# Linear attention and a Mish feed-forward: q loaded whole by halves of the heads, later loads and weight stores rearranged, two PSUM banks swapped

## The chip, the cores and the metric

The kernel runs on one core of one Trainium2 chip. The time is device microseconds of one execution; the median over several executions counts. Between two kernels, 0.3% is about what a measurement of this kernel can tell.

## The reference

q, k and v are float32, 8 batches by 8 heads by 576 positions by 64. The attention has no softmax; each head's 64 x 64 product of k and v is applied to q, and each row is divided by its root mean square. The result, as 4608 tokens by 512, goes through a feed-forward layer. Its weights w_in (512 x 2048) and w_out (2048 x 512) come as float64; all else is float32.

```
kv  = einsum('bhsd,bhse->bhde', k, v)
out = einsum('bhsd,bhde->bhse', q, kv)
x   = out / sqrt(mean(out*out, -1) + 1e-6) * g_norm
x   = x.transpose(0, 2, 1, 3).reshape(4608, 512)
h   = x @ w_in
sp  = where(h > 20, h, log1p(exp(min(h, 20))))
g   = h * tanh(sp)
return g @ w_out
```

## The kernel before

**The two large products.** x @ w_in and g @ w_out are each computed block by block as a scheme of seven products in place of eight (PROD, L22): the left operand has seven forms (A11, S1, S2, S4, A12, S3, A22, sums and differences of its quarters), the weights have seven (T1, T3, T2, T4, B11, B21, B22). Every form is split into a high and a low part in the reduced float32 type fp32r (split, L120 to L122: ScalarE casts the high part, VectorE subtracts to get the low one), and each product is three matmuls. Tokens go in 9 tiles of 512. A tile of part one has 28 slots, 7 products times 4 groups of columns; mm_in (L526) issues a slot's matmuls and put_in (L545) adds up the results, applies Mish (ScalarE, L118) and stores g to DRAM (gd) from GpSimd's queue. Part two reads g back (g_load, L731), makes its forms (g_form, L748) and multiplies them by w_out's (mm_out, L771). Its first half tile is different: its seven products go by pairs of chunks into four banks of their own (L855 to L875).

**Weights.** The float64 words are converted on the chip. weight_forms (L128) returns seven steps that the order calls by number: LOAD, SCALE (ScalarE, L142), JOIN (three VectorE operations, L147 to L149), DIFF (L157 to L159), BLOCKS and SUMS (the splits), and STORE. w_in's forms stay in SBUF as wf0 to wf7. w_out's are made in 16 halves during part one: weight_out (L192) converts one half in the tile wst, which has one buffer, and stores it (L200) to DRAM, in wod. In part two they are read back, as wo_load (L727).

**The order.** Nothing is scheduled automatically. The program text sets each engine's order: plan and evict are tables of calls by slot number (at, then, slot, L474 to L488), and the head of the kernel, which prepares the first tile, is written out (L592 to L648). SP issues nearly all loads in that order and waits in order; its transfers use eight lanes (DMAHW0 to 7 in the lists below), and an issue waits for the transfer that used the lane eight before. GpSimd's have eight of their own (DMASW).

**The head.** Tokens of the first tiles are handled by two units of four heads (u = 0 and 1). rows_load (L293) loads q, transpose (L318) turns it on TensorE, turned (L336) copies it to SBUF, kv_first_product (L228) and kv_keep (L266) make the k and v product, project (L354) applies it, sums (L391), rstd (L409) and normalize (L431) do the norm. rows[0] holds four consecutive tokens per partition, so that a run is 1 KB; spots (L289) picks the partitions of a segment.

## Time and profile before

| | |
|---|---|
| runs of the kernel | 878.30, 880.26, 880.67 us, median 880.26 |
| profiled execution | 880.55 us |
| its span, first to last instruction | 878.8 us |
| mean granted clock of TensorE | 0.987 |
| TensorE busy | 835.3 us, 95%, 7132 matmuls |
| VectorE busy | 608.8 us, 69% |
| ScalarE busy | 465.0 us, 53% |
| GpSimd busy | 78.5 us, 9% |
| moved by DMA | 175.54 MB, mean 200 GB/s |

The profile is of one execution. Busy times are shares of the span; an engine's idle time counts only where another waits for it. Start times in the timeline are microseconds from the span's start, and a bracket at a row's end gives the idle time of that engine just before it and the instruction whose end released it. The granted clock is given as a share of the full 2.4 GHz: 0.50 is 1.2 GHz.

### The profile page before, as it was taken

The numbers are of one execution on the slowest core, as the hardware profiler recorded it, in microseconds if no ns is written. First come the engines' busy times: TensorE is split into PE (matmuls) and PEld (weight loads), VectorE is DVE, ScalarE is ACT, GpSimd is POOL, SyncE is SP. The second block draws the span as 40 slices with busy tenths as digits, with TensorE's granted clock in tenths as the row PEclk, the third lists the DMA queues.
The fourth block names the chain that finished last, engine by engine and source line by source line (L and its number), as shares of the span: only waits on it lengthen the run. The fifth ranks groups of instructions, "written<-read, shape, count | busy, mean of one in ns | idle before, by whom it ended". The sixth has DMA issues, their size and how long they took to land.

```text
span 878.8 us, 17412 instructions
## 1 busy us (share of the span) xinstructions
PE 835.3 (95%) x7132; PEld 804.6 (92%) x7132; DVE 608.8 (69%) x804; ACT 465.0 (53%) x703; POOL 78.5 (9%) x133
## 2 busy tenths in 40 slices
PE   4679998999999999999999989999999999999997
PEld 4467998989999999999899979999999999999997
DVE  3899666877777686777763577677666777776772
ACT  3677666655665757666665443444444334334441
POOL 2001111111111111111112100000000000000000
PEclk9999999999999999999999989999999999999999
DMA  9964887979878695858377992444444443344421
GB/s 311 255 195 137 241 254 238 296 234 277 272 218 279 210 291 173 279 171 243 138 235 293 422 399 81 149 151 149 124 129 135 121 120 121 120 123 148 151 62 48
DMA packets 140320, 175.54 MB, mean 200 GB/s; under 512 B 16272, under 2 KB 117648, under 8 KB 139216
## 3 DMA queue, kind: packets, MB, share of 16 engines
q1 hardware_dynamic: 129232, 136.67, 50.7%
q0 software_dynamic: 11008, 37.76, 11.4%
q8 instruction: 56, 0.92, 0.4%
q14 instruction: 24, 0.20, 0.1%
HBM read 112.39 MB, written 62.00 MB: 198 GB/s over the span
## 4 chain that ended last, share of the span: by engine, by line
PE 73%; ACT 8%; DVE 7%; DMA 6%; issue 4%; SPq 1%; ACTq 0%; DVEq 0%
PE a L775 22%; PE bc L775 17%; PE a L532 16%; PE bc L532 11%; PE s L252 2%; DMA wf<-wod 2%; DMA wod<-wst 1%; DVE fa L122 1%; DVE ur L553 1%; DMA wf<-in_q_dram 1%; PE q L871 1%; ACT L417 1%; ACT L118 1%; DVE gf L385 1%; PE x L329 1%
## 5 line engine op out<-in xcount | busy, mean ns | idle before, releaser
L775 PE MATMUL a<-wf,gf 128*128 128x256 f32 x1632 | 201.8, 283 | 0.5 <-DVE ur L814 0.5
L775 PEld LDWEIGHTS a<-wf,gf 128*128 128x128 f32 x1632 | 198.4, 192 | 0.7 <-DVE ur L814 0.7
L122 DVE TENSOR_TENSOR gf<-g,gf 128x1024 fp32r<-128x1024 f32 (+1 forms) x123 | 132.9, 1087 | 92.5 <-ACT gf L121 92.4
L532 PE MATMUL a<-gf,wf 128*128 128x256 f32 x1296 | 174.1, 288 | 11.1 <-DVE gf L435 4.6
L532 PEld LDWEIGHTS a<-gf,wf 128*128 128x128 f32 x1296 | 163.8, 194 | 18.2 <-DVE gf L435 5.4
L532 PE MATMUL bc<-gf,wf 128*128 128x256 f32 x1296 | 171.6, 285 | 0.1
L532 PEld LDWEIGHTS bc<-gf,wf 128*128 128x128 f32 x1296 | 162.5, 192 | 1.9 <-DVE gf L122 0.7
L121 ACT CAST gf<-g 128x1024 fp32r<-128x1024 f32 (+1 forms) x123 | 114.5, 939 | 86.9 <-DVE g L755 65.5
L775 PE MATMUL bc<-wf,gf 128*128 128x256 f32 x1224 | 152.4, 283 | 0.0
L775 PEld LDWEIGHTS bc<-wf,gf 128*128 128x128 f32 x1224 | 149.3, 192 | 0.0
L532 PE MATMUL a<-a,wf 128*128 128x256 f32 x432 | 59.3, 287 | 0.8 <-DVE ur L553 0.8
L532 PEld LDWEIGHTS a<-a,wf 128*128 128x128 f32 x432 | 55.5, 193 | 3.8 <-DVE ur L553 1.0
L118 ACT ACTIVATE ur<-ur 128x1024 f32<-128x1024 f32 x36 | 38.1, 1058 | 37.1 <-DVE ur L553 37.1
L122 DVE TENSOR_TENSOR fa<-fl,fh 128x1024 fp32r<-128x1024 f32 x28 | 34.2, 1222 | 18.4 <-ACT fh L121 16.3
L122 DVE TENSOR_TENSOR gf<-gf 128x512 fp32r<-128x512 f32 x45 | 30.4, 689 | 24.0 <-ACT gf L121 24.0
L121 ACT CAST gf<-a 128x1024 fp32r<-128x1024 f32 x17 | 17.9, 1050 | 53.8 <-DVE a L752 53.8
L121 ACT CAST gf<-gf 128x512 fp32r<-128x512 f32 x45 | 27.1, 619 | 33.2 <-DVE gf L456 19.1
L509 ACT COPY ur<-a 128x512 f32<-128x512 f32 (+1 forms) x53 | 27.3, 516 | 32.6 <-PE a L775 26.5
L556 POOL DMA_DIRECT2D gd<-ula x36 | 26.3, 731 | 190.6 <-ACT ula L118 139.5
L553 DVE TENSOR_TENSOR ula<-bc,ula 128x512 f32<-128x512 f32 x36 | 24.7, 687 | 24.1 <-PE bc L532 23.9
L500 ACT COPY ur<-bc 128x512 f32<-128x512 f32 (+1 forms) x53 | 27.5, 518 | 26.4 <-PE bc L775 24.9
L551 POOL DMA_DIRECT2D gd<-ulb x36 | 25.6, 712 | 116.0 <-ACT ulb L118 104.6
(141 smaller groups left out, 937.0 us busy)
## 6 DMA issues: line engine op xcount, KB each, us to landing
g<-gd SPq DMA_DIRECT2D x18, 2048.0 KB, 15.7
gd<-ur POOLq DMA_DIRECT2D x36, 512.0 KB, 4.8
wod<-wst SPq DMA_DIRECT2D x16, 896.0 KB, 9.9
wf<-wod SPq DMA_DIRECT2D x8, 1792.0 KB
gd<-ula POOLq DMA_DIRECT2D x36, 256.0 KB, 5.0
gd<-ulb POOLq DMA_DIRECT2D x36, 256.0 KB, 4.5
w<-in_moe_w_out_dram SPq DMA_DIRECT2D x32, 256.0 KB, 5.9
km<-in_k_dram SPq DMA_DIRECT2D x28, 256.0 KB, 3.4
```

The lines of the kernel that those rows point to most:

```text
L118: nc.scalar.activation(o, i, AF.Mish)
L121: nc.scalar.copy(hi, src)
L122: nc.vector.tensor_sub(lo, src, hi.bitcast(F32))
L252: nc.tensor.matmul(kvps[o * D:(o + 1) * D, b % 2, h0 // 2 + i, :], kt, vt, start=(c == 0), stop=(c == CM))
L329: nc.tensor.matmul(ps[a][o * D:(o + 1) * D, c * P:(c + 1) * P], src, ident, start=True, stop=True)
L500: then(t + 2, lambda: nc.scalar.copy(dst(st, "22"), st["c"]))
L509: then(t + 4, lambda: nc.scalar.copy(dst(st, "12"), st["a"]))
L532: nc.tensor.matmul(bank[:, jj], w[:, right, a, kc, :], xf[:, b, kc, :], start=first and jj == kc == s == 0, stop=(kc == 1 and s == 2), ski ...
L551: at(t + 2, lambda: eng.dma_start(left[:, :, TH:T], o))
L553: nc.vector.tensor_add(o, bank, o)
L556: at(t + 3, lambda: eng.dma_start(left[:, :, 0:TH], o))
L775: nc.tensor.matmul(bank, gf[:, a, c, :], wo[c][:, right, b, :], start=first and c == s == 0, stop=(c == NF2 - 1 and s == 2), skip_group_ch ...
```

## The change

1. q of the first two tiles is laid out by whole blocks of 128 tokens, one token per partition and block. A transfer then has runs of 64 values; for the first tile there are four per half of the heads (rows_load takes the block c and the heads). The transposes become eight whole 128 x 128 ones per unit in place of sixteen of half the width, and project reads contiguous columns. The output rows of these tiles are stored 128 at a time.
2. The order of the head: q's second half and the second halves of k and v are issued ahead of the second weights; the second unit's transposes follow the first k and v product; the third weights' JOIN stands after the second unit's normalization; in part one's first slots the form S3 and kv_keep change places.
3. The banks of the first norm's sums and of the second unit's projection are exchanged ("a" and "bc").
4. w_out's forms are kept in DRAM and SBUF as two halves of 128 columns, the half outermost. A half is then one contiguous run of 7168 bytes per partition, and it is stored from GpSimd's queue in place of SP's. In part two each matmul's moving operand is two runs of 128 columns.
5. The load of g for the second half tile is issued behind the last two blocks of w_out's forms.

```diff
-    wod = [tc.dram_tile([P, 7, 2, G], F32, name=f"wod{c}") for c in range(NF2)]
+    wod = [tc.dram_tile([P, 2, 7, 2, P], F32, name=f"wod{c}") for c in range(NF2)]
...
-            nc.sync.dma_start(wod[c][:, :, :, h * P:(h + 1) * P], f.rearrange("p f s m n -> p f s (m n)").bitcast(F32))
+            nc.gpsimd.dma_start(wod[c][:, h], f.rearrange("p f s m n -> p f s (m n)").bitcast(F32))
...
-    def rows_load(j):
+    def rows_load(j, c, h0, n):
         for b, s0, cols in segments(j):
-            p = spots(cols)
-            src = q[b, 0:1, s0:s0 + 1, :]
-            src = bass.AP(src.tensor, src.offset, [[TR * D, p.stop - p.start], [S * D, H], [1, TR * D]])
-            nc.sync.dma_start(rows[j][p], src)
+            t0, t1 = max(cols.start, c * P), min(cols.stop, (c + 1) * P)
+            if t0 < t1:
+                src = q[b, h0:h0 + 1, s0 + t0 - cols.start:s0 + t0 - cols.start + 1, :]
+                src = bass.AP(src.tensor, src.offset, [[D, t1 - t0], [S * D, n], [1, D]])
+                nc.sync.dma_start(rows[j][t0 - c * P:t1 - c * P, c, h0 * D:(h0 + n) * D].rearrange("p (h d) -> p h d", d=D), src)
...
+                    h = 4 * u + 2 * a
                     for c in range(TR):
-                        for o in range(2):
-                            src = rows[j][:, 4 * u + 2 * a + o, c * D:(c + 1) * D]
-                            nc.tensor.matmul(ps[a][o * D:(o + 1) * D, c * P:(c + 1) * P], src, ident, start=True, stop=True)
+                        nc.tensor.transpose(ps[a][:, c * P:(c + 1) * P], rows[j][:, c, h * D:(h + 2) * D], ident)
...
-                st["x"] = [bank_new("a").rearrange("p m t -> p (m t)") for _ in range(2)]
+                st["x"] = [bank_new("bc").rearrange("p m t -> p (m t)") for _ in range(2)]
...
-                    ps = bank_new("bc").rearrange("p m t -> p (m t)") if u == 0 else ps_t.tile([P, T], F32, name="ss") if a == 0 else kvps.rearrange("p b n d -> p (b n d)")
+                    ps = bank_new("a").rearrange("p m t -> p (m t)") if u == 0 else ps_t.tile([P, T], F32, name="ss") if a == 0 else kvps.rearrange("p b n d -> p (b n d)")
...
-    rows_load(0)
+    for c in range(TR):
+        rows_load(0, c, 0, 4)
     kv0 += [wfp.tile([P, NKC, 9 * D], F32, name=f"wf{n}") for n in (3, 4)]
     kv_first(first)
+    for c in range(TR):
+        rows_load(0, c, 4, 4)
+    kv_first(second)
     weights(1, LOAD)
-    kv_first(second)
...
-    for f, n in ((S2, 0), (A12, 1), (S4, 2), (S3, 3), (A22, 5)):
+    for f, n in ((S2, 0), (A12, 1), (S4, 2), (S3, 4), (A22, 5)):
...
-    at(4, lambda: kv_keep(1, slice(0, NKC)))
+    at(3, lambda: kv_keep(1, slice(0, NKC)))
...
-        wo[c] = wfp.tile([P, 7, 2, G], F32R, name=f"wf{c}")
+        wo[c] = wfp.tile([P, 2, 7, 2, P], F32R, name=f"wf{c}")
...
-                    bank, gf[:, a, c, :], wo[c][:, right, b, :],
+                    bank, gf[:, a, c, :], wo[c][:, :, right, b, :],
...
-    at(t8 + 26, lambda: g_load(1))
...
     at(t, lambda: [wo_load(c) for c in range(NF2 - 2, NF2)])
+    at(t, lambda: g_load(1))
```

The lists below give an engine's instructions in program order: the line, the operation, written tile, read tiles and shape, how often in a row, and, in brackets, whom it waits for.

SP in the head, before: wf_139 of q goes whole, and the second weights (wf_145) stand ahead of the second halves of k and v.

```order
L137 DMA w_136<-in_moe_w_in_dram 128x4x256 x2
L298 DMA wf_139<-in_q_dram 128x8x256
L226 DMA wf_141<-in_k_dram 128x2x576
L226 DMA wf_142<-in_v_dram 128x2x576
L137 DMA wf_145<-in_moe_w_in_dram 128x4x256 x2
L226 DMA wf_141<-in_k_dram 128x2x576
L226 DMA wf_142<-in_v_dram 128x2x576 [waits DMAHW0_49]
```

The same with the change:

```order
L137 DMA w_136<-in_moe_w_in_dram 128x4x256 x2
L295 DMA wf_139<-in_q_dram 128x4x64 x4
L226 DMA wf_144<-in_k_dram 128x2x576
L226 DMA wf_145<-in_v_dram 128x2x576
L295 DMA wf_139<-in_q_dram 128x4x64 [waits DMAHW0_49]
L295 DMA wf_139<-in_q_dram 128x4x64 [waits DMAHW1_49]
L295 DMA wf_139<-in_q_dram 128x4x64 [waits DMAHW2_49]
L295 DMA wf_139<-in_q_dram 128x4x64 [waits DMAHW3_49]
L226 DMA wf_144<-in_k_dram 128x2x576 [waits DMAHW4_49]
L226 DMA wf_145<-in_v_dram 128x2x576 [waits DMAHW5_49]
L137 DMA wf_154<-in_moe_w_in_dram 128x4x256 [waits DMAHW6_49]
L137 DMA wf_154<-in_moe_w_in_dram 128x4x256 [waits DMAHW7_49]
```

Eight issues of q stand where one did, and the second weights (here wf_154) come behind all of k, v and q of the first tile.

VectorE in the head, before: from the second weights' differences (L157 to L159) past the first unit's normalization (L435, of x) and the third weights' JOIN (wf_152) to the second unit's normalization (L435, of the banks a).

```order
L157 TENSOR_TENSOR wd<-fl 128x512
L158 TENSOR_TENSOR wd<-fl,wd 128x256
L159 TENSOR_TENSOR wd<-fl,wd 128x256
L122 TENSOR_TENSOR wf_290<-fl,wf_290 128x256
L122 TENSOR_TENSOR wf_290<-fl,wf_290 128x2x256
L122 TENSOR_TENSOR wf_290<-wd,wf_290 128x4x256
L435 SCALAR_TENSOR_TENSOR gf<-x_281,gcol,fa 128x512 x2
L122 TENSOR_TENSOR gf<-gf 128x512
L147 TENSOR_SCALAR fl<-fl 128x1024
L148 SCALAR_TENSOR_TENSOR fl<-wf_152,fl 128x1024
L149 SCALAR_TENSOR_TENSOR fl<-wf_152,fl 128x1024
L435 SCALAR_TENSOR_TENSOR gf<-a,gcol,fh 128x512 x2
```

With the change, whose lines are lower by five (L430 is the normalization, wf_154 holds the second weights' words), the end of the second weights' JOIN and what follows:

```order
L149 SCALAR_TENSOR_TENSOR fl<-wf_154,fl 128x1024
L430 SCALAR_TENSOR_TENSOR gf<-x_267,gcol,fa 128x512 x2
L157 TENSOR_TENSOR wd<-fl 128x512
L158 TENSOR_TENSOR wd<-fl,wd 128x256
L159 TENSOR_TENSOR wd<-fl,wd 128x256
```

and some rows further, from the second weights' last splits to the third weights' JOIN (wf_159):

```order
L122 TENSOR_TENSOR gf<-gf 128x512
L122 TENSOR_TENSOR wf_332<-wd,wf_332 128x4x256
L430 SCALAR_TENSOR_TENSOR gf<-bc,gcol,fh 128x512 x2
L448 TENSOR_TENSOR s_125<-gf 128x512
L449 TENSOR_TENSOR gf<-gf 128x2x256
L122 TENSOR_TENSOR gf<-s_125,gf 128x512
L147 TENSOR_SCALAR fl<-fl 128x1024
L148 SCALAR_TENSOR_TENSOR fl<-wf_159,fl 128x1024
L149 SCALAR_TENSOR_TENSOR fl<-wf_159,fl 128x1024
```

The first unit's normalization moved ahead of the second weights' differences, and the third weights' JOIN moved from ahead of the second unit's normalization to behind it.

SP at the boundary of the parts, before: g is a half tile's Mish result read back, wf6 and wf7 (here wf_5905 and wf_5907) are the last two blocks of w_out's forms.

```order
L729 DMA wf_5722<-wod_107 128x3584 [waits PE_49]
L729 DMA wf_5843<-wod_108 128x3584 [waits PE_49]
L729 DMA wf_5845<-wod_109 128x3584 [waits PE_49]
L734 DMA g<-gd_95 128x16x256 [waits DMASW7_49,DMASW5_49,DMAHW6_49,DMASW2_49,Pool_49]
L729 DMA wf_5905<-wod_110 128x3584 [waits DMAHW7_49,PE_49]
L729 DMA wf_5907<-wod_111 128x3584 [waits DMAHW0_49,PE_49]
```

With the change:

```order
L723 DMA wf_5823<-wod_109 128x3584 [waits DMASW7_49,DMASW3_49,PE_49]
L723 DMA wf_5881<-wod_110 128x3584 [waits DMASW5_49,DMASW1_49,PE_49]
L723 DMA wf_5883<-wod_111 128x3584 [waits DMASW7_49,DMAHW1_49,DMASW3_49,PE_49]
L728 DMA g<-gd_95 128x16x256 [waits DMAHW2_49,Pool_49]
L728 DMA g<-gd_96 128x16x256 [waits DMASW4_49,DMAHW3_49,DMASW0_49,DVE_49]
```

The second load of g moved from ahead of the last two blocks to behind them. GpSimd's queue, with the change, around the first two stores of w_out's forms, which before were on SP:

```order
L551 DMA gd_96<-ula 128x2x256 [waits DMASW6_49,Activation_49]
L200 DMA wod_104<-wst 128x1792 [waits DMASW7_49,DVE_49]
L554 DMA gd_96<-ur 128x1024 [waits DMASW0_49]
L546 DMA gd_96<-ulb 128x2x256 [waits DMASW1_49,Activation_49]
L551 DMA gd_96<-ula 128x2x256 [waits DMASW2_49,Activation_49]
L200 DMA wod_104<-wst 128x1792 [waits DMASW3_49,DVE_49]
```

A store stands behind the store of g from ula and ahead of the one from ur, and waits for VectorE.

## Rows read from the trace of the kernel before

**Rows 1.** Waits of ScalarE: who, for whom, us in total, times, longest.

```profile
ACT wst L121 <- DMA wod<-wst: 9.4, 2, 5.0
```

**Rows 2.** Timeline of the head, TensorE and VectorE (start, us, engine, line, operation).

```profile
10.90 3.68 PE L329 MATMUL x<-ident,wf 128*64 128x128 f32 x32 [10.90 <-DMA wf<-in_q_dram]
...
36.73 0.49 PE L532 MATMUL a<-gf,wf 128*128 128x256 f32 x1 [4.56 <-DVE gf L435]
...
21.33 0.69 DVE L147 TENSOR_SCALAR fl<-fl 128x1024 uint32<-128x1024 uint32 x1 [2.21 <-ACT fl L142]
...
29.68 1.41 DVE L435 SCALAR_TENSOR_TENSOR gf<-x,gcol,fa 128x512 f32<-128x512 f32 x2 [1.16 <-ACT fa L414]
32.20 0.69 DVE L122 TENSOR_TENSOR gf<-gf 128x512 fp32r<-128x512 f32 x1 [1.10 <-ACT gf L121]
```

**Rows 3.** Windows: us, busy (instructions) of PE, PEld, DVE, ACT, POOL; PEclk, DMA share, GB/s.

```profile
2.00:17.00 15.00, 6.10 (x64) 6.13 (x64) 6.30 (x9) 4.03 (x6) 5.09 (x20) 1.00 0.99 335
36.00:66.00 30.00, 23.09 (x216) 20.32 (x216) 27.78 (x43) 19.50 (x30) 0.75 (x1) 0.89 0.67 205
129.50:134.50 5.00, 5.00 (x42) 5.00 (x41) 1.79 (x5) 2.61 (x6) 0.71 (x1) 1.00 0.98 297
197.30:200.60 3.30, 3.30 (x18) 3.30 (x17) 0.22 (x1) 3.23 (x4) 0.00 (x0) 0.50 0.92 311
508.00:525.00 17.00, 12.62 (x96) 12.45 (x95) 13.63 (x26) 6.69 (x16) 0.30 (x1) 0.90 1.04 403
```

**Rows 4.** Timeline of SP, VectorE, ScalarE and TensorE around stores of w_out.

```profile
124.77 5.58 SPq L316 DMA_DIRECT2D qs<-in_q_dram  x8
...
134.46 0.61 SPq L200 DMA_DIRECT2D wod<-wst  x1
...
128.84 0.69 DVE L122 TENSOR_TENSOR wst<-w,wst 128x512 fp32r<-128x512 f32 x1
...
140.79 0.61 ACT L121 CAST wst<-wx 128x128 fp32r<-128x128 f32 x2 [4.34 <-DMA wod<-wst]
...
142.88 1.70 PE L532 MATMUL a<-gf,wf 128*128 128x256 f32 x12 [1.24 <-ACT ula L495]
...
148.93 1.34 PE L532 MATMUL a<-gf,wf 128*128 128x256 f32 x9 [1.47 <-ACT ur L509]
...
196.33 0.86 PE L532 MATMUL a<-gf,wf 128*128 128x256 f32 x5 [1.90 <-ACT ula L495]
```

**Rows 5.** Timeline at the boundary of the parts: SP, ScalarE, VectorE, TensorE.

```profile
502.05 9.82 SPq L729 DMA_DIRECT2D wf<-wod  x2
...
517.90 1.04 ACT L121 CAST gf<-g 128x1024 fp32r<-128x1024 f32 x1 [0.60 <-PE q L871]
...
526.07 1.23 DVE L122 TENSOR_TENSOR gf<-g,gf 128x1024 fp32r<-128x1024 f32 x1 [1.19 <-ACT gf L121]
...
528.77 0.42 DVE L901 TENSOR_TENSOR ur<-q,ur 128x256 f32<-128x256 f32 x1 [1.48 <-ACT ur L900]
...
535.39 1.23 DVE L122 TENSOR_TENSOR gf<-g,gf 128x1024 fp32r<-128x1024 f32 x1 [1.17 <-ACT gf L121]
...
522.23 7.97 PE L871 MATMUL q<-wf,gf 128*128 128x256 f32 x42 [4.38 <-DMA wf<-wod]
...
538.68 5.92 PE L775 MATMUL bc<-wf,gf 128*128 128x256 f32 x48
```

**Rows 6.** DMA packets: a stretch with short ones, then one with longer ones.

```profile
DMA packets 102, 0.03 MB, mean 290 GB/s; under 512 B 94, under 2 KB 102, under 8 KB 102
...
DMA packets 55, 0.06 MB, mean 402 GB/s; under 512 B 0, under 2 KB 55, under 8 KB 55
```

**Rows 7.** DMA issues of the page: count, KB each, median us to landing.

```profile
gd<-ur POOLq DMA_DIRECT2D x36, 512.0 KB, 4.8
```

**Rows 8.** Chain of waits in order of time, 66 to 80 us: start, us, what.

```profile
71.63 1.81 PE ss L404 x4
...
76.52 1.95 PE x L365 x8
```

More of the change, by code (lines that the diff above doesn't have):

```diff
@@ L363, in project @@
                     if j < T32:
-                        o, r = (t.rearrange("p (c n) -> p c n", n=P)[:, :, spots(c)] for t in (ps, st["q"][:, a]))
-                        nc.tensor.matmul(o, kvf[b][:, hp, :], r, start=True, stop=True)
+                        nc.tensor.matmul(ps[:, c], kvf[b][:, hp, :], st["q"][:, a, c], start=True, stop=True)
                         continue
@@ L595, in linear_attention_rms_mish_ffn @@
     t = wfp.tile([P, 3, 2 * T], F32, name="wf2")
[L596 to L597 removed]
+    rows[0], turned_q = t[:, 0:2].rearrange("p a (c n) -> p (a c) n", c=TR // 2), t[:, 2].rearrange("p (a t) -> p a t", a=2)
+    for c in range(TR):
+        rows_load(0, c, 0, 4)
     kv0 += [wfp.tile([P, NKC, 9 * D], F32, name=f"wf{n}") for n in (3, 4)]
     kv_first(first)
+    for c in range(TR):
+        rows_load(0, c, 4, 4)
+    kv_first(second)
     weights(1, LOAD)
[L601 removed]
     for r in (slice(0, D), slice(D, P)):
@@ L617, in linear_attention_rms_mish_ffn @@
     weights(0, SCALE, JOIN, DIFF)
-    do(0, 0, "transpose")
-    do(0, 1, "transpose")
-    weights(0, BLOCKS)
-    do(0, 0, "turned")
-    do(0, 1, "turned")
-    weights(0, SUMS)
+    do(0, 0, "transpose", "turned")
+    weights(0, BLOCKS, SUMS)
     kv_first_product(first)
     kv_keep(0, first)
+    do(0, 1, "transpose", "turned")
+    do(0, 0, "project", "square")
     weights(1, SCALE, JOIN)
-    do(0, 0, "project", "square")
-    weights(1, DIFF, BLOCKS)
     kv_first_product(second)
@@ L632, in linear_attention_rms_mish_ffn @@
     do(0, 1, "project")
+    do(0, 0, "rstd", "normalize")
+    weights(1, DIFF, BLOCKS)
+    do(0, 1, "square")
+    x_form(A11)
     weights(1, SUMS)
-    do(0, 0, "rstd")
+    do(0, 1, "sums", "rstd", "normalize")
+    weights(2, SCALE)
+    x_form(S1)
     k_load(1, 0)
     k_load(1, 1)
-    rows[1] = att.tile([P, H, TR * D], F32, name="qs")
-    rows_load(1)
-    do(0, 1, "square", "sums")
-    weights(2, SCALE)
-    do(0, 0, "normalize")
-    x_form(A11)
-    weights(2, JOIN)
-    do(0, 1, "rstd", "normalize")
-    x_form(S1)
-    weights(2, DIFF)
+    rows[1] = att.tile([P, TR, H * D], F32, name="qs")
+    for c in range(TR):
+        rows_load(1, c, 0, H)
+    weights(2, JOIN, DIFF)
     weights(4, LOAD)
     weights(5, LOAD)
-    for f, n in ((S2, 0), (A12, 1), (S4, 2), (S3, 3), (A22, 5)):
+    for f, n in ((S2, 0), (A12, 1), (S4, 2), (S3, 4), (A22, 5)):
         at(n, lambda f=f: x_form(f))
@@ L789, in o_store @@
         if i < T32:
-            for b, s0, cols in segments(i):
-                p = spots(cols)
-                row = b * S + s0 + half * G // P
-                dst = out[row:row + 1, :]
-                dst = bass.AP(dst.tensor, dst.offset, [[TR * DM, p.stop - p.start], [DM, G // P], [1, DM]])
-                nc.sync.dma_start(dst, st["o"][p])
+            for r in range(G // P):
+                c = half * G // P + r
+                for b, s0, cols in segments(i):
+                    t0, t1 = max(cols.start, c * P), min(cols.stop, (c + 1) * P)
+                    if t0 < t1:
+                        row = b * S + s0 + t0 - cols.start
+                        nc.sync.dma_start(out[row:row + t1 - t0, :], st["o"][t0 - c * P:t1 - c * P, r, :])
             return
```

5 lines of the change are left out of this document (1 added, 4 removed).

## Prediction

> **What bounds the kernel now.** I read the page first: TensorE is busy nearly throughout (95% in the table of the page), so only the places where it stands still, or runs at a lower clock, can give time back. The lists of waits name three such places: VectorE's normalization ahead of the first product, a store of w_out's forms, for which ScalarE waits twice, 9.4 us together [rows 1], and w_out's forms at the start of part two. The timeline shows how each comes about.
>
> *The head.* The first product starts at 36.73, after 4.56 us of waiting for the second unit's normalization [rows 2], which stands behind the JOIN of the third weights in VectorE's order. That looks like so much to be had. But from 36 to 66 us VectorE is busy for 27.78 us of 30 and TensorE for 23.09 [rows 3]: whatever the first product gains, the weights' conversion that the later products wait for still goes at VectorE's pace. So the head is worth what VectorE's own waits are worth.
>
> *The stores of w_out's forms.* SP issues in order: eight q loads from 124.77, then other loads, then the store at 134.46, though VectorE had written the forms by 128.84 + 0.69 = 129.53 [rows 4]. The staging tile has one buffer, so ScalarE's next cast waits 4.34 us until 140.79, its evictions come late behind it, and TensorE waits 1.24 and 1.47 us [rows 4]. At the next place it waits 1.90 us, and then the granted clock is 0.50 (1.2 instead of 2.4 GHz) from 197.3 to 200.6 [rows 3, 4], which costs half of 3.3 us. Together 1.24 + 1.47 + 1.90 + 1.65 = 6.3 us.
>
> *The boundary of the parts.* TensorE waits 4.38 us at 522.23 for w_out's last two blocks, which SP issued from 502.05 on [rows 5], with the 2 MB of g for the second half tile just ahead of them. The DMA engines are busy throughout (share 1.04, 403 GB/s from 508 to 525) [rows 3].
>
> **The change part by part.** *Head, -0.7 us.* Removed: VectorE's waits of 1.16 us (29.68, for the reciprocal root) and 1.10 us (32.20, for a cast) [rows 2]; in the new order the first normalization stands before the differences of the second weights, which fill such waits. I count 0.4 us of new waits between steps that now follow each other closely, so -1.9. Added: the second words w1 now land behind all of q, k and v of batch 0. That is w0 1.05, q 1.05, k and v 2.36 and w1 1.05, 5.5 MB. From 2 to 17 us the rate is 335 GB/s [rows 3], 5.0 MB, so 5.5 MB are in at 18.5. q's runs fall from 1 KB to 256 B: packets of under 512 B go at 290 GB/s, those of 1 to 2 KB at 402 [rows 6], so its 1.05 MB take 3.6 instead of 2.6 us, 19.5. From the end of the transfer by this reckoning to the JOIN I allow 2.9 us, ScalarE's scaling among them: w0 and q, 2.1 MB, would be in at 8.3, and TensorE starts on q at 10.90 [rows 2], 2.6 later. So the JOIN of w1 starts at 22.4 instead of 21.33 [rows 2]: +1.1. Sum -0.8, and I take -0.7. Ends: -2.3, all of both waits gone and w1 no later; and +1.7, if half of the 4.9 us that seven more issues of q take on SP (5.58 / 8 = 0.7 each [rows 4]) pushes w1 back as well. The 4.56 us are not counted a second time: with bank bc free for the second unit the first product can start earlier, but the second and third products then wait longer. The transposes on TensorE shrink from 32 instructions per unit pair to 16; TensorE has nothing else to do there, so 0. The output rows of the first two tiles are stored in other pieces: SP and the DMA are half idle in part two, 0.
>
> *Stores from GpSimd, -5.0 us.* GpSimd's queue holds only the stores of g. The new store waits there for 129.53 and holds back the store of g behind it for some microseconds; nobody waits for that one soon, since its tile has two buffers. Landing: a 512 KB store from GpSimd's queue takes 4.8 us [rows 7]; the 896 KB of a half, scaled by size, 8.4; the old store, issued at 134.46, had landed by 140.7 [rows 4], 6.2. I take 6.2, the same bytes: it lands at 135.7. ScalarE asks for the tile at 140.79 - 4.34 = 136.45, so its wait is gone; at 8.4 the store lands at 137.9 and 1.5 of 4.34 us stay. Of the 6.3 us I leave the 1.24, since ScalarE's work there is otherwise unchanged and dense, and take -5.0. Ends: -6.3, and 0 if the store lands no sooner. The other stores cost nothing now: ScalarE waited for two only [rows 1].
> What speaks against it is a row: from 129.5 to 134.5 the DMA engines are already 98% busy at 297 GB/s [rows 3]. An earlier issue gains only if the two queues share them; at half of 297 the 0.92 MB take 6.2 us, which agrees with my value. The Trainium skill, "DMA: Bandwidth & Descriptors", section "Issuing engines are not separate DMA queues", says that queues of different issuers run on the same 16 engines, so that spreading transfers over issuers saves only issue time. By that page the sum would be nearer to +0.8 than to -4.2; the trace can't decide it, because no store of this size went through GpSimd's queue.
>
> *The boundary, +1.5 us.* w_out's last blocks no longer have g in front, so the 4.38 us go. What is late next is g itself: the DMA engines carry the same bytes, full until 525 [rows 3], so g lands at about 525. What the boundary costs then shows in when the later products run. The first form of the second half tile then starts on ScalarE at 525 instead of 517.90, and the forms follow at VectorE's pace. From the first start (517.90) to the end of the third form, S2 (526.07 + 1.23) is 9.4 us [rows 5]: 534.4. Then VectorE combines the first half tile's sums in 7 additions, 3.1 us, and makes the fourth form, 1.2, and the fifth, S4, with its difference and the cast, 3.5: from 528.77 to the end of S4's form at 536.62 it takes the 7.8 us of these three [rows 5]. S4 is ready at 542.2, and with 0.5, an allowance of mine, its product runs at 542.7. In the trace of before the two products A12 and S4 start at 538.68 and take 5.92 [rows 5], so S4 starts 2.9 later, at 541.6. So +1.1; and 0.4 for a clock that may fall in the new wait, as it did in the old. Ends: -6.1 if g is in time and only the old stall goes, 4.38 and the clock lost around it (a mean of 0.90 over 17 us, 1.7 us) [rows 3]; +5 if g is so late that the new wait is as long as the old, with its clock.
>
> *The moving operand in part two, 0.* w_out's blocks are kept as two halves, so each of the 17 x 168 = 2856 products of the later half tiles, and the 168 of the first, streams two runs of 128 instead of 256 in one. The nearest rows: 2048 columns in runs of 512 take 1.81 us, and 2048 columns cut into 32 short strided runs 1.95 [rows 8]. That is at most 0.14 us for 24 boundaries, 5.8 ns each; 3024 of them give +17.6 as the upper end. The two groups also differ in the number of weight loads (4 and 8), which explains the 0.14 by itself, so I take 0.
>
> **Sum:** -0.7 - 5.0 + 1.5 + 0 = -4.2. The profiled execution took 880.55, which is 0.29 above the median of 880.26; 880.55 - 4.2 = **876.3 us**.
>
> **The rivals.** *R1, the store gains nothing.* The engines are full from 129.5 on [rows 3], the store issued earlier lands when it lands now, and ScalarE waits as before. -0.7 + 0 + 1.5 gives 881.3. For it: the share of 0.98. Against it: the store stands behind 14 earlier issues on SP, and a queue of its own need not. The Trainium skill's section named above would make it so. *R2, slower: the two-run operand costs.* If each of the 3024 products pays for its boundary, 4.2 / 3024 = 1.4 ns eat the whole gain; at 2.9 ns, half the upper end, it is +8.8, or 885.1. For it: the two groups allow it [rows 8]. Against it: the weight loads explain them. *R3, the new wait at the boundary is long:* +5 instead of +1.5, 879.8. For it: the engines are full there. *R4, no new wait there:* g lands early enough, -6.1 instead of +1.5, 868.7. For it: g is only 2 MB of the traffic. Against it: it stands last in its queue.
> That the change does nothing is ruled out: SP's and GpSimd's orders differ in every place named.
>
> **How the numbers follow.** My forecast 0.55, with a range of its own from 873.5 (the store's wait gone entirely, head -2.2) to 878.8 (a third of the stores' gain missing, +1.7, and the head at +0.1); R1 0.20, R2 0.08, R3 0.09, R4 0.08. The range from 870.5 to 882.5 holds all of the forecast, R1 and R3 and leaves out R2, most of R4 and the tails. A measurement here tells 0.3%, 2.6 us, from no change. Faster by more, below 877.6: 0.46 of the forecast's 0.55, and R4's 0.08: 0.54. Within it: 0.08 of the forecast, 0.16 of R1 and 0.06 of R3: 0.30. Slower: R2's 0.08, 0.04 of R1, 0.03 of R3 and 0.01: 0.16.
>
> **What would show it.** Head: w1's JOIN at 22 to 23 and the first product some 5 us earlier, but the products of the second tile's start moved by less than 2 us. Stores: issued on GpSimd's queue at about 129.5 and landed before 136.5, no wait of ScalarE for the store in the list, no granted clock of 0.50 near 198. If the wait for the store is still there, R1 holds. Boundary: no wait for w_out's forms, but one of TensorE on a form of the second half tile at 530 to 543. If there is none, R4. Operand: the mean of part two's products does not move; if it grows by 2 ns or more, R2 holds. I am wrong if the sum moves for a reason outside these four places, above all if the first tile's products are slowed by loads that now come later.

## The result, and the profile after

The changed kernel takes 882.33 us in the median of 15 runs, the kernel before 880.23 in 15; the ratio of the two is 1.0024, with a 95% interval from 1.0013 to 1.0035. It is slower, by some 2 us and by less than the 0.3% that I had called no change, where I had forecast 4 us less. The profiled execution has a span of 880.9 us; before it was 878.8, so the two traces differ by what the runs differ.

Where did it go? A row that both kernels have 53 times marks the flow of the products: ScalarE's copy of a sum (L509 before, L504 after). The timeline of ScalarE, before, in five places (start, us, engine, line, operation):

```profile
130.41 0.59 ACT L509 COPY ur<-a 128x512 f32<-128x512 f32 x1 [0.84 <-PE a L532]
...
226.13 0.58 ACT L509 COPY ur<-a 128x512 f32<-128x512 f32 x1
...
455.54 0.58 ACT L509 COPY ur<-a 128x512 f32<-128x512 f32 x1
467.65 0.59 ACT L509 COPY ur<-a 128x512 f32<-128x512 f32 x1
...
559.04 0.37 ACT L509 COPY ur<-a 128x256 f32<-128x256 f32 x1 [1.56 <-PE a L775]
```

and the same five in the changed kernel:

```profile
131.88 0.59 ACT L504 COPY ur<-a 128x512 f32<-128x512 f32 x1 [0.84 <-PE a L527]
...
223.98 0.58 ACT L504 COPY ur<-a 128x512 f32<-128x512 f32 x1
...
452.94 0.59 ACT L504 COPY ur<-a 128x512 f32<-128x512 f32 x1
467.31 0.59 ACT L504 COPY ur<-a 128x512 f32<-128x512 f32 x1
...
561.04 0.37 ACT L504 COPY ur<-a 128x256 f32<-128x256 f32 x1 [1.20 <-PE a L769]
```

In this pair of profiles the head costs 1.5 us (130.41 to 131.88). The two places with the w_out stores give 3.6 back (from 1.5 behind to 2.1 ahead at 226). Some 0.4 more comes by 456, then 2.3 are lost between 456 and 468 alone, and 2.3 more at the boundary of the parts. From 559 to 861 us the distance does not move by 0.05 us: part two's products are as fast as before. 1.5 - 3.6 - 0.4 + 2.3 + 2.3 = 2.1.

**Head.** The timeline of ScalarE, VectorE and TensorE, changed kernel:

```profile
20.82 1.02 ACT L370 ACTIVATE fa<-x 128x1024 f32<-128x1024 f32 x1 [3.09 <-PE x L360]
21.74 1.14 ACT L142 ACTIVATE fl<-wf 128x1024 f32<-128x1024 f32 x1
...
22.91 0.69 DVE L147 TENSOR_SCALAR fl<-fl 128x1024 uint32<-128x1024 uint32 x1 [3.18 <-ACT fl L142]
...
57.90 0.69 DVE L147 TENSOR_SCALAR fl<-fl 128x1024 uint32<-128x1024 uint32 x1 [0.35 <-ACT fl L142]
...
31.31 1.58 PE L527 MATMUL a<-gf,wf 128*128 128x256 f32 x11 [1.09 <-DVE gf L122]
...
46.99 1.12 PE L252 MATMUL s<-vm,km 128*64 128x64 f32 x16 [5.65 <-DMA vm<-in_v_dram]
```

The JOIN of the second weights starts at 22.91 where it was 21.33 [rows 2], because ScalarE scales them (L142) right behind the square of the first unit (L370). The first products come 5 to 7 us earlier than the 36.73 of before, and TensorE then stands still for 5.65 us at 46.99, for a load of v: the start moved, the pace did not. q's short runs go at 251 GB/s (the DMA view from 5.6 to 7.2 us, in q's first half):

```profile
DMA packets 1622, 0.40 MB, mean 251 GB/s; under 512 B 1612, under 2 KB 1622, under 8 KB 1622
```

**Stores.** The timeline of GpSimd, ScalarE and TensorE at the two places:

```profile
131.41 0.57 POOL L200 DMA_DIRECT2D wod<-wst  x1 [7.09 <-DVE wst L122]
...
140.48 0.61 ACT L121 CAST wst<-wx 128x128 fp32r<-128x128 f32 x2 [2.56 <-DVE wx L149]
...
143.64 1.28 ACT L412 ACT_TABLE_LOAD   x1
...
146.30 1.28 ACT L118 ACT_TABLE_LOAD   x1
...
148.08 0.58 ACT L504 COPY ur<-a 128x512 f32<-128x512 f32 x1
...
148.72 3.13 PE L527 MATMUL a<-gf,wf 128*128 128x256 f32 x24 [1.28 <-ACT ur L504]
...
200.58 2.66 PE L527 MATMUL a<-gf,wf 128*128 128x256 f32 x20 [1.26 <-ACT ur L504]
```

and the page's row of these stores (count, KB each, median us to landing):

```profile
wod<-wst POOLq DMA_DIRECT2D x16, 896.0 KB, 5.4
```

The store is issued 0.4 us after VectorE's last part of the forms (131.00), where it was 4.9 us after it before [rows 4], and lands 5.5 us later. The page of before has 9.9 for the landing, but that is the last of the 16 stores, the only one whose landing that trace shows. By the packets of the two traces the old store at the first place ended 5.7 us after its issue and the new one 5.1, so nearly all that was saved there is the time of issue. The layout changed together with the queue (packets of 7168 B instead of 512 B), and no run separates the two; where little else moves, the last packet of a store ends 3.5 us after the issue with the change and 4.6 before.

ScalarE waits for the store nowhere; at 140.48 it waits for VectorE. But a wait of TensorE of 1.3 us for ScalarE's copy L504 remains at both places. That copy (148.08) stands behind two table loads, for the norm and back for Mish, 1.28 us each at 143.64 and 146.30. At the first place it is the 1.47 us of before [rows 4]; at the second it came out from under the store's wait.

**The last tile's norm.** SP, GpSimd and VectorE between 443 and 455 in the changed kernel, and under it the same rows of the kernel before:

```profile
443.03 0.29 SPq L417 DMA_DIRECT2D rd<-fl  x1
445.36 1.26 SPq L424 DMA_DIRECT2D fh<-rd  x2
446.67 1.28 SPq L424 DMA_DIRECT2D fa<-rd  x2
...
447.46 0.57 POOL L200 DMA_DIRECT2D wod<-wst  x1 [1.37 <-DVE wst L122]
...
454.97 1.22 DVE L432 TENSOR_TENSOR gf<-gf,fa 128x1024 f32<-128x1024 f32 x1 [2.80 <-DMA fa<-rd]
```

```profile
445.59 0.29 SPq L422 DMA_DIRECT2D rd<-fl  x1
447.17 1.26 SPq L429 DMA_DIRECT2D fh<-rd  x2
448.47 1.28 SPq L429 DMA_DIRECT2D fa<-rd  x2
449.85 0.59 SPq L200 DMA_DIRECT2D wod<-wst  x1
...
455.32 1.23 DVE L437 TENSOR_TENSOR gf<-gf,fa 128x1024 f32<-128x1024 f32 x1 [0.34 <-DMA fa<-rd]
```

From the store of the reciprocal roots (rd) to VectorE's second multiplication it takes 9.7 us before and 11.9 after, and VectorE waits 2.80 us for the loads instead of 0.34. The loads are issued 2.3 us after the store of rd instead of 1.6, and w_out's last store is now on another queue, beside them, and not behind them.

**Boundary.** SP, ScalarE and TensorE in the timeline:

```profile
502.83 0.55 SPq L728 DMA_DIRECT2D g<-gd  x1
...
526.18 1.04 ACT L121 CAST gf<-g 128x1024 fp32r<-128x1024 f32 x1 [9.21 <-DMA g<-gd]
...
528.54 5.49 PE L769 MATMUL a<-wf,gf 128*128 128x256 f32 x24 [5.77 <-DVE gf L122]
...
543.49 1.79 PE L769 MATMUL bc<-wf,gf 128*128 128x256 f32 x13 [0.56 <-DVE gf L122]
```

and the window behind it (us, busy and instructions of PE, PEld, DVE, ACT and POOL, PEclk, DMA share, GB/s):

```profile
528.00:534.00 6.00, 5.46 (x25) 5.46 (x26) 5.14 (x5) 1.76 (x2) 0.00 (x0) 0.50 0.42 134
```

The wait for w_out's last blocks [rows 5] is gone, and TensorE waits 5.77 us for the second half tile's first form, whose load of g landed at about 526. Behind that wait the granted clock is 0.50, and the product takes 5.49 us for 24 matmuls instead of 3.04 (f1 below). Four products later, at 543.49, TensorE waits once more, 0.56 us, for the fifth form, S4 (0.47 to 0.56 in all seven kernels with this order of loads). So the time lost at half clock in between is not what the boundary costs: what counts is when S4 is ready. Its product started at 541.6 before.

### The profile page after: what moved, and what is told of

It is laid out like the page before. It is cut to its first block, busy times and chain, and to the rows that moved or that the text cites. A ratio compares the mean times of both kernels' runs of the same rounds, so it can differ in the third digit from the quotient of the medians.

```text
span 880.9 us, 17243 instructions
## 1 busy us (share of the span) xinstructions
PE 834.1 (95%) x7036; PEld 801.6 (91%) x7036; DVE 608.7 (69%) x804; ACT 464.4 (53%) x703; POOL 87.4 (10%) x149
## 4 chain that ended last, share of the span: by engine, by line
PE 67%; DVE 10%; ACT 9%; DMA 7%; issue 4%; SPq 1%; DVEq 0%; ACTq 0%
PE a L769 22%; PE bc L769 16%; PE a L527 14%; PE bc L527 9%; DMA g<-gd 3%; PE s L252 2%; DVE ur L548 1%; DVE fa L122 1%; ACT L412 1%; DMA qs<-in_q_dram 1%; DMA rd<-fl 1%; DVE gf L122 1%; DVE gf L380 1%; ACT gf L121 1%; DMA fa<-rd 1%
## 5 line engine op out<-in xcount | busy, mean ns | idle before, releaser
L769 PE MATMUL a<-wf,gf 128*128 128x256 f32 x1632 | 204.2, 285 | 6.3 <-DVE gf L122 5.8
L769 PEld LDWEIGHTS a<-wf,gf 128*128 128x128 f32 x1632 | 200.7, 194 | 6.7 <-DVE gf L122 6.0
L504 ACT COPY ur<-a 128x512 f32<-128x512 f32 (+1 forms) x53 | 27.3, 516 | 30.7 <-PE a L769 24.6
```

The source lines that it names most:

```text
L504: then(t + 4, lambda: nc.scalar.copy(dst(st, "12"), st["a"]))
L769: nc.tensor.matmul(bank, gf[:, a, c, :], wo[c][:, :, right, b, :], start=first and c == s == 0, stop=(c == NF2 - 1 and s == 2), skip_group ...
```

## The experiments

All were timed beside the kernel before in five rounds. The table has each kernel's ratio to before and, from its profile, how far the marker row above moved against the profile of before within four stretches (us; minus is a gain). Between 468 and 496 and from 559 on no kernel moved by more than 0.05.

| kernel | ratio, 95% interval | to 130 | 130 to 226 | 456 to 468 | 496 to 559 |
|---|---|---|---|---|---|
| the change | 1.0024, 1.0013 to 1.0035 | +1.5 | -3.6 | +2.3 | +2.3 |
| e1, g as before | 1.0010, 1.0001 to 1.0018 | -0.1 | -3.6 | +2.1 | -0.5 |
| e2, last store on SP | 1.0022, 1.0010 to 1.0033 | +0.7 | -3.7 | +1.4 | +2.3 |
| e3, S3 in slot 3 | 1.0017, 1.0005 to 1.0030 | -0.9 | -3.7 | +1.8 | +2.2 |
| e4, second weights earlier | 1.0043, 1.0030 to 1.0056 | +2.9 | -3.7 | -0.1 | +2.4 |
| f1, g first | 0.9929, 0.9913 to 0.9945 | -0.9 | -3.7 | +2.1 | -6.8 |
| f2, scaling first | 1.0045, 1.0031 to 1.0059 | +0.1 | -3.7 | +1.9 | +2.2 |
| f3, before + w_out part | 0.9973, 0.9964 to 0.9982 | +0.4 | -3.3 | +0.4 | -0.8 |
| f4, before + banks | 1.0006, 0.9993 to 1.0020 | -0.3 | 0.0 | -0.2 | -0.8 |
| h1, f1 + S3 in slot 3 | 0.9904, 0.9891 to 0.9917 | -2.2 | -3.7 | +1.8 | -6.5 |
| h2, f3 + g first | 0.9888, 0.9874 to 0.9902 | 0.0 | -3.4 | 0.0 | -5.4 |
| h3, before + g first | 0.9936, 0.9925 to 0.9948 | -0.3 | +1.5 | -0.1 | -5.9 |
| h4, before + head | 1.0023, 1.0008 to 1.0038 | +1.2 | +1.9 | +0.4 | -0.7 |
| i1, eight small loads | 1.0047, 1.0033 to 1.0060 | 0.0 | -3.7 | +1.9 | +2.2 |
| i2, last store later | 1.0019, 1.0010 to 1.0029 | +0.7 | -3.7 | +0.5 | +2.3 |

Kernels with the same head differ by up to 2.4 us at 130 in single profiles (the change, e1, e2, f1, i1 and i2: +1.5, -0.1, +0.7, -0.9, 0.0, +0.7), so that column tells only what lies outside that. The column to 226 has such a scatter too: h3 and f4 run the code of before in that stretch and stand at +1.5 and 0.0. The stretch from 226 to 456 is not in the table: it brings -0.8 to +0.1 in ten of the kernels, and costs more in e3 (2.1), i1 (1.1), i2 (1.0), h4 (0.9) and h1 (0.6). And the change was timed in another session than its variants, with before's median at 880.23 and in theirs at 878.51 to 879.48, so small differences between two ratios tell little: e4, f2 and i1 have the change's own median, 882.3 to 882.5, and ratios of 1.0043 to 1.0047.

**e1: g's load.** One line moved back:

```diff
-    at(t, lambda: g_load(1))
+    at(t8 + 26, lambda: g_load(1))
```

> The changed kernel with one part undone: the load of g for the second half tile is issued ahead of w_out's last two blocks again. In the changed kernel TensorE waits 5.77 us at 522.8 for the second half tile's first form, and part two runs 2.3 us later against the kernel before than part one's end did. Theory (g comes last and is late): the wait on the form goes, a wait for w_out's last blocks of some 4.4 us comes back at 518, and the time falls by about 2.3 us, to 880.0. Rival (the bytes decide, whichever transfer stands last): the wait only changes its name and the time stays within 0.8 us of the changed kernel's 882.3.

The boundary costs 0.5 less than in the profile of before instead of 2.3 more, and the old wait is back: 

```profile
520.86 7.11 PE L866 MATMUL q<-wf,gf 128*128 128x256 f32 x42 [4.75 <-DMA wf<-wod]
```

The order of the loads matters, then. The ratio fell by 0.0014, 1.2 us, with intervals that overlap, so its size rests on the profiles. e1, f3, f4 and h4 all have the order of before there and stand at -0.5 to -0.8: the one profile of before was slow at the boundary by that much, and the change's cost is nearer to 3 us.

**e2: the last store.**

```diff
-            nc.gpsimd.dma_start(wod[c][:, h], f.rearrange("p f s m n -> p f s (m n)").bitcast(F32))
+            eng = nc.sync if 2 * c + h == 2 * NF2 - 1 else nc.gpsimd
+            eng.dma_start(wod[c][:, h], f.rearrange("p f s m n -> p f s (m n)").bitcast(F32))
```

> The changed kernel with one store moved: the last of the 16 stores of w_out's forms is issued from SP, behind the loads that spread the last tile's norm, as before; the other 15 stay on GpSimd. Theory (issued at 447.5 from GpSimd, this store shares the DMA engines with those loads, the last normalization starts at 455.0 and the products near 460 come 2.3 us later): the spread lands some 2.5 us earlier and the time falls by 2.3 us, to 880.0. Rival (the 2.3 us come from VectorE's and ScalarE's own order there, or from this one execution): no change within 0.8 us, and the second load of the spread lands as late as now.

Between the two: 1.4 is lost near 460 instead of 2.3. The store may have a part in it, not all, and the time did not move by more than its interval.

**e3: the place of kv_keep.**

```diff
-    for f, n in ((S2, 0), (A12, 1), (S4, 2), (S3, 4), (A22, 5)):
+    for f, n in ((S2, 0), (A12, 1), (S4, 2), (S3, 3), (A22, 5)):
...
-    at(3, lambda: kv_keep(1, slice(0, NKC)))
+    at(4, lambda: kv_keep(1, slice(0, NKC)))
```

> The changed kernel with one part undone: the form S3 is made in slot 3 and the second batch's kv_keep in slot 4 again. Theory (with kv_keep first, ScalarE's scaling of the fifth weights comes later and VectorE waits four times, 1.0 us in all, between 54.3 and 58): those waits go, the products after 66 us come 1.0 us earlier, 881.3. Rival (the later second weights alone make the head late, and the waits only show it): the products after 66 us stay within 0.3 us of the changed kernel's.

VectorE's next JOIN starts without a wait, at 55.69 instead of 57.90:

```profile
55.69 0.69 DVE L147 TENSOR_SCALAR fl<-fl 128x1024 uint32<-128x1024 uint32 x1
```

Measured from the JOIN before it (46.32 here, 46.46 in the change) to the one after it (65.70, 67.14) that is 1.3 us. The theory holds in the trace up to 130 us (and again in h1 against f1, -2.2 and -0.9); the total shows 0.6 us, inside the intervals. In e3's profile 2.1 us are lost again between 226 and 456: at 358.17 VectorE waits 3.38 us for a norm's second load, as the changed kernel does in the last tile.

**e4 and f2: what starts the second weights' JOIN.** e4 issues the weights earlier, f2 calls their scaling earlier:

```diff
-    kv_first(second)
-    weights(1, LOAD)
+    weights(1, LOAD)
+    kv_first(second)
```

> The changed kernel with one load moved: the second weights are issued ahead of the second halves of k and v (still behind all of q). Theory (w1 behind 5.5 MB is what starts its JOIN at 22.91 instead of 21.33): the JOIN starts by 21.3 and VectorE runs 0.4 to 1.2 us earlier from there to 66 us, so the time falls by about as much, to 881.5. Rival (ScalarE's copies ahead of the scaling, or VectorE's wait for the first norm, hold it): the JOIN starts earlier, the normalization of the first unit waits longer by the same, and the time does not move by more than 0.3 us.

```diff
-    do(0, 0, "project", "square")
-    weights(1, SCALE, JOIN)
+    weights(1, SCALE, JOIN)
+    do(0, 0, "project", "square")
```

> The changed kernel with the second weights' SCALE and JOIN called ahead of the first unit's projection and square. Theory (the second weights have landed by some 20.3 us, but ScalarE scales them only at 21.74, behind the square that waits for TensorE): the JOIN starts at 21.4 to 21.7 instead of 22.91, and VectorE runs 0.5 to 1.2 us earlier up to 75 us, 881.4. Rival (the square, now behind the scaling, delays the sums and the first norm): the first normalization waits longer by what the JOIN gained, and the time does not move by more than 0.3 us.

In e4 the JOIN starts at 22.28 and in f2 at 21.82, so both started it earlier; but what stands behind it, the first unit's normalization (L430), then waits 2.78 us in e4 and 1.71 in f2, where it waited 0.67:

```profile
28.27 1.41 DVE L430 SCALAR_TENSOR_TENSOR gf<-x,gcol,fa 128x512 f32<-128x512 f32 x2 [2.78 <-ACT fa L409]
```

```profile
26.74 1.41 DVE L430 SCALAR_TENSOR_TENSOR gf<-x,gcol,fa 128x512 f32<-128x512 f32 x2 [1.71 <-ACT fa L409]
```

(e4 first, then f2.) In f2 the rival held: the JOIN is 1.1 us earlier, the norm waits 1.0 longer and starts where it did, at 26.74 against 26.79. In e4 it came worse than that: the JOIN is 0.6 us earlier and the norm 1.5 later, since the second halves of k and v now come behind the weights. The new order put the norm between the JOIN and the differences, so the JOIN's start alone brings nothing. Neither is faster than the change.

**f1: g first.**

```diff
-    at(t, lambda: g_load(1))
+    at(t8 + 8, lambda: g_load(1))
```

> The changed kernel with the load of g for the second half tile issued right behind that for the first, some 457 us in, ahead of all of w_out's blocks. Theory (from 474 to 531 SP's queue is full at 410 to 430 GB/s and serves in order, so whichever of g and the last blocks is last comes late; between 462 and 473 it is nearly empty): g lands by 470, w_out's last two blocks land by 518.5 as in the changed kernel, neither is waited for, and part two starts 4.5 to 5.5 us earlier than in the changed kernel, 877.3. Rival (the tile's room is released late, or part one's stores suffer): SP waits with g, all of w_out's blocks come later behind it, and nothing or less than 1 us is gained.

More than expected: 6.8 us ahead of before over the boundary, 9.1 ahead of the change. That is about what R4 gave for g in time, 6.1. SP issues both loads of g from 453.62 on, and the second half tile's first product starts 8.3 us earlier than in the change, 2.6 of them from part one, at the full clock:

```profile
453.62 3.58 SPq L728 DMA_DIRECT2D g<-gd  x2
...
520.29 3.04 PE L769 MATMUL a<-wf,gf 128*128 128x256 f32 x24
```

**f3 and f4: parts alone.** Both start from the kernel before. f3 takes the lines of the w_out part, of which these are two (the others are the shapes of wod and wo, and the first half tile's operand); f4 exchanges the banks.

```diff
-            nc.sync.dma_start(wod[c][:, :, :, h * P:(h + 1) * P], f.rearrange("p f s m n -> p f s (m n)").bitcast(F32))
+            nc.gpsimd.dma_start(wod[c][:, h], f.rearrange("p f s m n -> p f s (m n)").bitcast(F32))
...
-                    bank, gf[:, a, c, :], wo[c][:, right, b, :],
+                    bank, gf[:, a, c, :], wo[c][:, :, right, b, :],
```

```diff
-                st["x"] = [bank_new("a").rearrange("p m t -> p (m t)") for _ in range(2)]
+                st["x"] = [bank_new("bc").rearrange("p m t -> p (m t)") for _ in range(2)]
...
-                    ps = bank_new("bc").rearrange("p m t -> p (m t)") if u == 0 else ps_t.tile([P, T], F32, name="ss") if a == 0 else kvps.rearrange("p b n d -> p (b n d)")
+                    ps = bank_new("a").rearrange("p m t -> p (m t)") if u == 0 else ps_t.tile([P, T], F32, name="ss") if a == 0 else kvps.rearrange("p b n d -> p (b n d)")
```

> The kernel before with only the w_out part of the change: the layout by halves, its stores from GpSimd, the two-run operand in part two. Theory (this part gains 3.3 us at the two places where ScalarE waited for a store, and some 0.3 by the way, and the operand costs nothing): 3.6 us less up to 226 us and no change in part two, ratio 0.996. Rival (what was gained comes from the later phase of the head, or is given back near 460): less than 1.5 us in all, ratio 0.998 or more.

> The kernel before with only the two banks exchanged. Theory (VectorE's pace sets the head): the first product starts 3 us or more earlier than 36.73, and the products from 66 us on move by less than 0.3 us; ratio 1.000. Rival (the first product's start carries through): the products from 66 us on come 1 us or more earlier.

f3 gains 3.3 us at the stores, keeps nearly all of it to the end, and its part two is as fast as before; the total is 0.9973, 2.4 us, less than the 0.996 expected. So this part alone is faster than the kernel before. In f4 the first product starts 4.1 us earlier and the time does not move, as forecast for the head:

```profile
32.61 1.58 PE L532 MATMUL a<-gf,wf 128*128 128x256 f32 x11 [0.34 <-DVE gf L122]
```

**h1 to h4: sums and the head alone.** h1 is f1 with the edit of e3, h2 is f3 and h3 is before, each with the load of g moved, in h2 and h3 as below; h4 is before with all of the change's head.

```diff
-    at(t8 + 26, lambda: g_load(1))
+    at(t8 + 8, lambda: g_load(1))
```

> The changed kernel with two edits: g for the second half tile loaded right behind that for the first, and S3 in slot 3, kv_keep in slot 4 as before. Theory (the two gains add): another 1.0 us below the kernel with the early g alone, ratio to the kernel before 0.992 to 0.9915. Rival (an earlier start of part one is given back where the last tile's norm waits for its loads): no better than the early g alone, 0.993.

> The kernel before, its head untouched, with the w_out part of the change and the early load of g. Theory (stores -3.3, boundary -4.5 to -5.5, and the 2 us that the changed kernels lose near 461 belong to the changed head and stay away): ratio 0.990 to 0.9915, and no late second load of the norm near 452. Rival (the changed head is worth something under the stores): no better than 0.993.

> The kernel before with one edit: g for the second half tile is issued right behind that for the first. Theory (SP's queue is full from 474 and in order, and nearly empty before): the wait of 4.4 us for w_out's last two blocks at 517 goes with its slow clock, nothing else moves up to 500 us, -4.5 to -5.5 us, ratio 0.994 to 0.995. Rival (the 2 MB collide with the last tile's loads and stores of part one): the products between 460 and 500 come later, and less than 3 us is gained.

> The kernel before with the head of the change alone: q by whole blocks and halves, the order of loads, the head's order and the banks; w_out's layout, its stores on SP and g's load as before. Theory (the head costs 0.3 us on the mean of four profiles and up to 1.5, kv_keep's place 1.0 of it, and the 2 us near 461 come with the head but only where a store shares the engines from GpSimd): +0.3 to +1.5 us up to 130 us, less than 1 us near 461, ratio 1.000 to 1.002. Rival (the 2 us near 461 are the head's alone): 2 us are lost near 461 here too, ratio 1.003 or more.

The gains add (f3's 2.4 us and h3's 5.6 against 9.8 in h2, within their intervals), and h2 is the fastest: 870.35 us, 1.1% under before and faster than the change by 1.4%. One moved line (h3) brings 0.64% of it. The head alone (h4) is slower by itself, by 2.0 us in the ratio. In its profile that is 1.2 us up to 130, inside the scatter, and 1.9 more by 226. There ScalarE waits for the store on SP for 11.2 us in all, against 9.4 in before and 10.3 in h3, whose code there is before's, so most of the 1.9 can be scatter. At the first place (4.34 before):

```profile
144.29 0.60 ACT L121 CAST wst<-wx 128x128 fp32r<-128x128 f32 x2 [6.61 <-DMA wod<-wst]
```

Near 461 it loses 0.4 only, and f3 0.4, h2 nothing: the 2 us there were seen only with the changed head and the stores on GpSimd together, though not in e4, which has both.

**i1 and i2: the loss near 461.** i1 adds to the change eight loads of 64 bytes on SP in the sixth tile, into tiles that nobody reads; i2 calls the last store four slots later.

```diff
+    def small_loads():
+        for n in range(8):
+            t = const.tile([1, 16], F32, name=f"small{n}")
+            nc.sync.dma_start(t, g_norm[0:16].rearrange("(o p) -> o p", o=1))
+    at(NS * 5 + 17, small_loads)
```

```diff
-            at(max(NS - 2, t + n), run)
+            at(max(NS - 2, t + n + (4 if s == 6 and i == len(places) - 1 else 0)), run)
```

> The changed kernel with eight loads of 64 bytes into tiles that nobody reads, issued on SP in the sixth tile (about 310 us in), so that every later instruction of SP stands at another place of its code. Theory (in the seven profiles that lose 1.3 to 2.3 us near 461, an 8 KB packet of the instruction queue falls within 0.1 us of the last norm's store and the loads that wait for that store are issued 0.7 us later than elsewhere; it is SP's code): the packet moves, the loads are issued 1.6 us after the store and not 2.3, and less than 1 us is lost near 461; 881. Rival (another engine's code, or no cause at all): the packet stays where it is, the loads are issued 2.2 to 2.4 us after the store and 1.8 to 2.3 us are lost again; 882.3.

> The changed kernel with the last of the 16 stores of w_out's forms called four slots later; it stays on GpSimd. Theory (the second loads of the spread, issued at 446.7, share the DMA engines with that store and land 2 us late): they land 1 to 2 us earlier and 0.3 to 1.0 us is lost near 461, of which the late issue is the rest; 881. Rival (the store has no part in it): the second normalization starts 11.5 to 12 us after the norm's store as now, and 1.8 to 2.3 us are lost; 882.3.

i1 changed nothing near 461: the loads are issued 2.4 us after the store of rd again, with the same 8 KB packet of the instruction queue just beside that store. So it is not SP's own place in its code. In i2 the loads are still issued 2.3 us after the store, but VectorE's second multiplication starts 1.8 us sooner after it (10.2 us instead of 11.9, waiting 1.28 instead of 2.80), and of the 2.3 us lost only 0.5 are left:

```profile
453.77 1.23 DVE L432 TENSOR_TENSOR gf<-gf,fa 128x1024 f32<-128x1024 f32 x1 [1.28 <-DMA fa<-rd]
```

So by i2 the last w_out store has 1.8 of the 2.3 us, by e2 0.9. Its total, 1.0019, does not stand apart from the change's 1.0024. The store alone does not do it. In the kernels with the stores on GpSimd one stands 4.4 us after the store of rd in each of the four tiles before too. Where the loads are issued in time, the second multiplication starts 9.9 us after the store of rd in the mean of those 48 cases, and 9.8 us in the 10 cases without a store of w_out near. In two cases, in f4 and h3 near 300 us, the loads are late by 1.2 and 1.4 us without such a store; there it starts after 11.2 and 11.0. So in the mean the store beside the loads costs nothing by itself (single cases run from 9.0 to 12.5), the late issue goes with the loss, and how the two act together is not shown. What makes the loads late by 0.7 us stays open.

## Why the prediction was wrong

The sum was -0.7 - 5.0 + 1.5 + 0 = -4.2, and by the profile it is +1.5 - 3.6 + 2.3 + 0, and 2.3 that it did not have, less 0.4. Of the 6.3 us between the two, the head has 2.2, the stores 1.4, the place that I put at nothing 2.3 and the boundary 0.8.

*Head: -0.7 forecast, +1.5 in the profile, +1.2 alone in h4, and about +0.4 on the mean of the seven profiles with this head.* The reading that VectorE's pace sets it was right: f4 starts the first product 4.1 us earlier for nothing. Two steps failed. "I count 0.4 us of new waits between steps that now follow each other closely" was too few: VectorE waits 0.67 and 0.70 us for the two norms, and kv_keep ahead of S3, a line of the diff that I read and did not price, costs 1.3 (e3). The two kernels without that exchange, e3 and h1, stand at -0.9 and -2.2, on the side that I had forecast. And the JOIN's start, right within half a microsecond (22.4 forecast, 22.91 measured), was luck: the weights' landing does not set it alone, for with the scaling called first (f2) the same order of loads gave 21.82, and e4 loaded them earlier and lost. At the 251 GB/s of its stretch q's 1.05 MB in 256 B runs come to 4.2 us by my estimate, not 3.6.

*Stores: -5.0 forecast, -3.6 measured, -3.3 alone (f3).* The mechanism was right: issued when VectorE is done, landed in 5.5 us against my 6.2, ScalarE's wait gone. R1, the store gains nothing, is refuted: the DMA engines were busy (a share of 0.95 from 131.4 to 137), but a queue of its own shared them. The rule of the Trainium skill ("DMA: Bandwidth & Descriptors", "Issuing engines are not separate DMA queues"), that another issuer saves only issue time, is not contradicted: what was saved here is issue time, 4.5 us behind SP's other loads. That the store would gain nothing did not follow from it. The mis-sized step is "Of the 6.3 us I leave the 1.24": a wait of 1.3 us is left at each of the two places, not at one, because ScalarE's table loads stand ahead of the copy at both; together 2.5 of the 6.3. How much less than 5.0 it is, one profile can't tell, since h3, with the code of before, is 1.5 slower there; in the totals f3 gains 2.4 us on before, and h2 4.2 on h3, from which it differs by this part alone.

*The last tile's norm: not in the sum, +2.3.* I wrote "The other stores cost nothing now" and looked only at who waits for a store, not at what a store on its own queue takes from the transfers that it had stood behind. The last one had been behind the norm's loads on SP; from GpSimd it goes beside them. That question I put only at the boundary. It is part of the answer only: f3, h2 and e4, with the same store from GpSimd, lose 0.4 us or nothing here. In the kernels that lose, the loads themselves are also issued 0.7 us late, and the cause of that is open.

*Boundary: +1.5 forecast, +2.3 in the profile, about 3 against four profiles with the old order.* The mechanism was right, and nearly the size: g landed at 526 (525 forecast), and the forms followed at VectorE's pace as I had counted, so that S4's product, for which TensorE does wait, started at 543.49 and not at 542.7. The mis-sized step is g's landing, 1.2 us late. I had not seen the wait of 5.77 us at the first form and the half clock from 528 to 534, but S4's wait comes behind them; the 0.4 that I allowed for the clock was not needed. Against before S4's product is 1.9 us late, and the changed kernel had come to 496 us 0.3 ahead: 2.3. R3 and R4 (+5 and -6.1) lie further off on either side, and R3's +5 does not follow from its condition: a new wait as long as the old one, in its place, would cost nothing. And I weighed the two orders against each other only; the queue was nearly empty from 466 to 474 (8 to 201 GB/s) and both loads of g could go ahead of w_out's blocks (h3, -5.9).

*Operand: 0 forecast, 0.0 measured* over the 302 us from 559 to 861, some 2500 products; R2 is refuted. f3 has the two-run operand without the rest and shows the same.

## What to carry to other kernels

Where one queue is full and serves in order, changing which transfer stands last only moves the wait, here to a dearer place; look for the stretch in which the queue is nearly empty and move the whole transfer there. A transfer that goes to a queue of its own starts earlier and also stops being behind the others: for each of its instances, not only those that are waited for, ask which loads it will now run beside. Count a "first product earlier" as nothing until the engine that sets the pace of the stretch has been found. And before a difference of 1 or 2 us in one profile is explained, look how far two profiles of the same code lie apart there: here it was 1.5.

## What the runs showed of the hardware

Transfers issued by SP were served one after another at the boundary: counted by packet size in stretches of 2 us, the changed kernel moves only w_out's blocks (14336 B packets, with the stores of g beside them) from 474 to 518 and only g (1024 B packets, two loads) from 519 to 531, though the first of these loads was issued at 502.83; but for 7 KB the two mixes overlap in one stretch of 2 us.

```
from us   g, KB (1024 B)   w_out blocks, KB (14336 B)   GB/s
514.0            0                   686                 425
516.0            7                   574                 406
518.0          578                    84                 368
520.0          684                     0                 350
522.0          680                     0                 348
```

A wait of TensorE of 5.8 us was followed by 6 us at a granted clock of 0.50, one of 1.67 us (h2, at 517.98) by none: there the next 21 matmuls took 2.77 us. And in the seven profiles of kernels with the changed head and the GpSimd stores that lost 1.4 to 2.3 us near 461, and in i1 and i2, an 8 KB packet of the instruction queue starts 0.7 us after the issue of the store of rd, within 0.1 us of its first data packet, and the loads that wait for that store come 2.2 to 2.4 us after it; in the others (before, e4, f3, f4, h2 to h4) it does not, and they come 1.6 us after. That they stand side by side does not make it the cause. In other tiles a 16 KB packet of that queue starts 0.5 to 0.9 us after the issue of a store of rd in six places: in three the loads come 2.8 to 3.0 us after it (f4, h1, h3), in three 1.6 (before, f3, h2). Whose packets they are, the trace does not say.
